# Retention, experts and feed-forward in one kernel: where the operands of the last six row tiles are made

## Chip, core and metric

One core of a Trainium2 chip runs the whole kernel. The metric is the device time of one execution in microseconds; the median of three runs before the change is 1802.8 us (1802.75 to 1803.73).

## What is computed

```python
# q, k, v: (4, 8, 576, 64)   retention with a decay per head
ret = (q @ k.T / 8) * Dmat            # Dmat[i, j] = gamma_h ** (i - j) for i >= j, else 0
x = (ret @ v), heads side by side     # (2304, 512)
# experts: w_gate (512, 8), w1 (8, 512, 1024), w2 (8, 1024, 512)
P = exp(x @ w_gate - max); 8 times: rows, then columns of P are brought to sum
out = sum over e of P[:, e] * (relu(x @ w1[e]) @ w2[e])
# feed-forward, 512 -> 2048 -> 512
h = out @ w_in;  result = max(0.01 * h, h) @ w_out
```

## The kernel before

**Two phases.** The retention walks through 20 chunks (lines 834 to 901): two batch pairs, five row chunks of 128, 128, 128, 128 and 64 rows, two batch halves. The loop behind it runs over 20 units of 512 hidden columns (16 of the experts, 4 of the feed-forward), and in each over three stages of 384 row pairs (three row tiles). A row tile j is a pair of 128-row blocks, one of each half; there are nine, index 0 to 8, and the ninth is put together from the 64-row chunks. Stage 0 takes tiles 0 to 2, stage 1 tiles 3 to 5, stage 2 tiles 6 to 8.

**Products with seven terms.** A block product of 2 by 2 is made from seven products instead of eight, each in three fp16 terms (high by high, high by low, low by high). So each row tile needs seven operands (four blocks of x and three sums), each as a high and a low fp16 part; `PROD` (line 40) names them 0 to 6, and `H_ORDER` (line 41) sets the order of the products of a stage, which take the operands in the order 0, 3, 6, 1, 5, 2, 4. `product_h` (L1028) makes the hidden part, in two column groups g of seven products each; the second products (L1199, L1241 for the first unit) trail and begin after the second stage.

**One step of the retention** (lines 838 to 900), for chunk n: GpSimd decays q of chunk n+2 (L671); TensorE makes the scores of chunk n+1 (`emit_qk`, L694), which VectorE decays (L697); TensorE adds the state's part (L711); `emit_scale` of chunk n-1 sums the absolute values of each row with products against ones (L754) and one more product of a single row that adds 2^-90 (L755), then VectorE makes a power of two of it (L765) and scales the output (L767) into a tile `op`; TensorE adds the chunk's own part (L721), ScalarE takes absolute values (L725); TensorE makes the state's increase (L739), ScalarE copies it (L744). The chunks of 64 rows (n = 8, 9, 18, 19) make no state, and those that open a batch pair (n = 0, 1, 10, 11) use none.

**Operands in the retention.** `emit_operands` (line 805) makes all of a tile in large pieces over the following steps: four sums (L816 to L819, on GpSimd, for tile index 7 on VectorE), two ScalarE casts (L824, three and four operands) and two VectorE subtractions (L826). Tiles 0 to 2 go straight into the operand ring in SBUF; tiles 3 to 7 go into a tile `xt` and by one DMA to DRAM (`keep_x`, L486). Only tile 8 goes through `operand_tasks` (line 515), a list of 14 small tasks: two of GpSimd (L532, L533 and L538, L539), and four times a high part (ScalarE or VectorE, L64), a low part (VectorE, L561) and a store.

**The ring.** It holds eight operands. The first stage's seven lie there from the start; `try_loads` (line 499) loads the next one (L510) when a place is free, all three tiles are stored, and the planner's clock is `LAND` = 4 us past the store. A place comes free after the second column group's product. `need_x` (line 1386) forces tasks and loads that are still missing when a product needs them.

**What sets the order.** In the retention it is written out by hand: `step()` (line 858), four times a chunk from chunk 4 on, issues at most one task of the first unit's W1 (`prep_steps`, line 188). In the loop the class `Order` (line 67) keeps six queues ("evac", "turn", "gate", "hid", "weights", "f64") and a planner's clock; `pump` issues what is ready in that order, "turn" before "weights". An engine's own instructions run in the order of issue; all DMAs go through SyncE's one queue, where one that waits holds those behind it.

**Weights.** A unit's raw W1 and W2 (1 MB each, `load_raw`, L186) are measured by ScalarE (L201), brought to a common power of two, scaled (L261) and split: high parts by ScalarE (L276, L305), sums and low parts by GpSimd (L286, L293, L311). For the first unit the maximum over the partitions is taken by products (`top` and `scale`, L234 and L245), and W1's second low parts are VectorE's (L311); W2 of the first unit is left to the loop. Later units go through VectorE transposes (`quarters`, `beside`, `turned`, `spread`). `float64_steps` (line 394) turns the feed-forward's float64 weights into float32 in the background of the loop; its first loads (L402) start when the ninth tile's four pieces are stored.

## Time and profile before

| what | value |
|---|---|
| median of 3 runs | 1802.8 us |
| profiled execution, its own time | 1801.8 us |
| its span | 1799.9 us |
| mean granted TensorE clock | 0.993 |
| TensorE matmul busy | 1765.2 us (98%) |
| VectorE, ScalarE, GpSimd busy | 83%, 71%, 45% |
| first product of the loop (L1028) | at 91.80 us |

The span runs from the first to the last instruction on the core; the execution's time has 1.9 us around it. Matmuls are pipelined and their ends are modelled, so TensorE's pace is read from the distance of two starts and not from busy time. A row of the order of time gives start, length, engine, line and what ended the idle time before it.

### The profile page before, as it was taken

To read this page: it belongs to the slowest core of one execution; us is meant where nothing else is said; L and a number is where in the kernel's file an instruction comes from. 1 tells how busy PE (TensorE), PEld (TensorE's weight loads), DVE (VectorE), ACT (ScalarE), POOL (GpSimd) and SP (SyncE) were. 2 spreads that over 40 slices of the span, in tenths; PEclk is the share of its full clock that TensorE was granted. 3 is DMA by queue.
4 is the path that set the end of the run, shared out by engine and by line. 5 is a ranking of instruction groups with operands and counts; after the bars stand their busy time and mean duration, and the time that the engine had idled before them with its cause. 6 is when DMAs were issued, how large, how long until landed. Compare 5 with 4: busy or idle time off the path is not lost.

```text
span 1799.9 us, 35885 instructions
## 1 busy us (share of the span) xinstructions
PE 1765.2 (98%) x13686; PEld 1290.1 (72%) x13686; DVE 1489.9 (83%) x2642; ACT 1285.3 (71%) x2808; POOL 815.8 (45%) x782
## 2 busy tenths in 40 slices
PE   9999999999999999999999999999999988999998
PEld 8855677777777777777777777777776555777776
DVE  7955898999888888888898888887776895788886
ACT  6777777777777777777777777777675666877653
POOL 4815362726344463626263444636224972443600
PEclk9999999999999999999999999999999999999999
DMA  9773545446354454454464454443443454444242
GB/s 345 271 252 103 152 127 170 136 150 187 115 171 138 156 156 152 127 170 151 135 190 120 163 147 156 147 143 102 140 150 103 158 170 129 131 125 141 78 128 83
DMA packets 206784, 272.98 MB, mean 152 GB/s; under 512 B 13698, under 2 KB 177556, under 8 KB 201492
## 3 DMA queue, kind: packets, MB, share of 16 engines
q1 hardware_dynamic: 206612, 270.70, 47.9%
q8 instruction: 107, 1.75, 0.4%
q14 instruction: 65, 0.53, 0.1%
HBM read 241.02 MB, written 29.63 MB: 150 GB/s over the span
## 4 chain that ended last, share of the span: by engine, by line
PE 88%; DVE 7%; POOL 2%; issue 1%; ACT 1%; DMA 1%; SPq 0%; DVEq 0%; POOLq 0%; ACTq 0%
PE s L1199 17%; PE hA L1028 12%; PE hB L1028 12%; PE hE L1028 12%; PE s1a L1199 11%; PE s1b L1199 11%; PE hD L1028 6%; PE s L1241 2%; PE s1a L1241 1%; PE s1b L1241 1%; DVE y L1212 1%; DVE xst L561 1%; POOL y L1338 1%; DVE hs L1119 0%; PE xo L721 0%
## 5 line engine op out<-in xcount | busy, mean ns | idle before, releaser
L1028 PEld LDWEIGHTS <-w 128*128 128x128 f16 x5040 | 492.5, 98 | 265.7 <-DMA xring<-x 3.9
L1199 PEld LDWEIGHTS <-hs 128*128 128x128 f16 x3888 | 380.9, 98 | 87.7 <-DVE hs L1119 4.7
L1199 PEld LDWEIGHTS <-hp 128*128 128x128 f16 x2916 | 285.6, 98 | 80.9 <-issue 2.9
L286 POOL TENSOR_TENSOR w<-raw,w 128x384 f16<-128x384 f32 x152 | 163.3, 1088 | 364.1 <-ACT w L276 363.8
L293 POOL TENSOR_TENSOR raw<-raw 128x256 f32<-128x256 f32 x304 | 280.4, 922 | 20.0
L1212 DVE SCALAR_TENSOR_TENSOR y<-s,fac,y 128x256 f32<-128x256 f32 (+1 forms) x322 | 197.6, 614 | 101.2 <-PE s L1199 84.1
L1028 PE MATMUL hE<-xring,w 128*128 128x384 f16 x1440 | 274.7, 326 | 5.3 <-DMA xring<-x 2.1
L1028 PE MATMUL hA<-xring,w 128*128 128x384 f16 x1440 | 276.5, 328 | 2.8 <-ACT w L276 2.3
L1028 PE MATMUL hB<-xring,w 128*128 128x384 f16 x1440 | 274.0, 326 | 0.0
L1199 PE MATMUL s<-w,hs 128*128 128x256 f16 x1932 | 264.2, 273 | 0.8 <-ACT s L1217 0.7
L1119 DVE TENSOR_TENSOR hs<-fs,hs 128x768 f16<-128x768 f32 (+1 forms) x228 | 241.4, 1062 | 8.3 <-ACT hs L1109 6.8
L311 POOL TENSOR_TENSOR w<-raw,w 128x512 f16<-128x512 f32 x148 | 200.4, 1368 | 76.5 <-ACT w L305 76.2
L1109 ACT ACTIVATE hs<-fs 128x768 f16<-128x768 f32 (+1 forms) x228 | 187.6, 823 | 44.4 <-DVE fs L1144 35.1
L446 POOL TENSOR_TENSOR f<-f,e 128x256 f32<-128x256 f32 x64 | 52.8, 825 | 352.5 <-DVE e L438 296.2
L1109 ACT ACTIVATE hp<-fp 128x384 f16<-128x384 f32 x240 | 160.4, 677 | 13.3 <-DVE fp L1067 12.5
L1212 DVE SCALAR_TENSOR_TENSOR y<-s1a,fac,y 128x256 f32<-128x256 f32 (+1 forms) x161 | 98.7, 613 | 50.9 <-ACT s L1217 28.7
L1199 PE MATMUL s1a<-w,hs 128*128 128x256 f16 x972 | 133.4, 273 | 4.6 <-ACT hs L1109 2.4
L1028 PE MATMUL hD<-xring,w 128*128 128x384 f16 x720 | 136.6, 326 | 1.1 <-ACT hD L1056 1.1
L1212 DVE SCALAR_TENSOR_TENSOR y<-s1b,fac,y 128x256 f32<-128x256 f32 (+1 forms) x161 | 98.7, 613 | 43.3 <-ACT s L1217 18.6
L1199 PE MATMUL s1b<-w,hs 128*128 128x256 f16 x960 | 132.1, 273 | 1.8 <-DVE hs L1119 1.4
L1199 PE MATMUL s1a<-w,hp 128*128 128x256 f16 x972 | 132.6, 273 | 1.1 <-DVE y L1212 1.0
L1199 PE MATMUL s1b<-w,hp 128*128 128x256 f16 x960 | 131.6, 274 | 0.5 <-DVE y L1212 0.5
(215 smaller groups left out, 2699.4 us busy)
## 6 DMA issues: line engine op xcount, KB each, us to landing
xring<-x SPq DMA_DIRECT2D x413, 384.0 KB
raw<-in_wm SPq DMA_DIRECT2D x32, 1024.0 KB
r<-in_wf SPq DMA_DIRECT2D x64, 256.0 KB
qk<-in_qk SPq DMA_DIRECT2D x16, 512.0 KB
vk<-in_vk SPq DMA_DIRECT2D x16, 512.0 KB
wf_s<-f SPq DMA_DIRECT2D x32, 256.0 KB
raw<-wf_s SPq DMA_DIRECT2D x8, 1024.0 KB
x<-xst SPq DMA_DIRECT2D x30, 256.0 KB
```

Source lines behind the costliest of these rows:

```text
L286: nc.gpsimd.tensor_tensor(v[0], v[1], v[2], op=ALU.subtract)
L293: nc.gpsimd.tensor_tensor(o, x, y_, op=ALU.subtract)
L311: (nc.gpsimd if u or part else nc.vector).tensor_tensor(lo, r, hi, op=ALU.subtract)
L446: nc.gpsimd.tensor_tensor(dst, dst, cur["tx"].bitcast(F32), op=ALU.mult)
L561: nc.vector.tensor_tensor(st[d][:, :, 1], src[d](), st[d][:, :, 0], op=ALU.subtract)
L1028: nc.tensor.matmul(bank, w[:, a, wi, k, :], x[:, :, b, k, :], start=r in (1, 5) and k == q == 0, stop=k == 1 and q == 2, skip_group_check= ...
L1109: nc.scalar.activation(hid[k][:, 0, a:b], src[:, a:b], AF.Relu if moe and relu else AF.Copy)
L1119: nc.vector.tensor_tensor(t[:, 1, a:b], src[:, a:b], t[:, 0, a:b], op=ALU.subtract)
L1199: nc.tensor.matmul(out_, t[:, a, i, ts], w[:, b, wi, 0, :], start=start and k == 0, stop=k == 5, skip_group_check=True)
L1212: nc.vector.scalar_tensor_tensor(out_, bank, f, out_, op0=ALU.mult, op1=ALU.add)
L1241: nc.tensor.matmul(bank, t[:, a, i, ts], w[:, b], start=l == g == q == 0, stop=l == g == 1 and q == 2, skip_group_check=True)
L1338: nc.gpsimd.tensor_scalar(y[i], y[i], st["s", j][:, h:h + 1], None, op0=ALU.mult)
```

## The change

It keeps the retention's outputs of tiles 3 to 8 in the tiles `y` of the final sum (allocated before the retention for these six), makes the operands of tiles 3 to 7 through `operand_tasks` in small pieces, of which `step()` issues one at every second call, and leaves the rest to the loop's queue "turn". The product of a single row gives way to a bias in ScalarE's absolute value. W1's and W2's maximum of the first unit goes the way of the later units, W1's second low parts go to GpSimd, and `step()` now issues W2's tasks too, with a closer pace for GpSimd and VectorE. The stores of tiles 0 to 2 from the ring wait until chunk 15. The next unit's raw weights load without waiting for stores, and the float64 steps start when all six tiles are stored.

```diff
         def total(p):
             def f():
-                nc.vector.reduce_sum(st["m"][:, p] if u == 0 else m32[:, p], st["mx"][:, p], axis=AX.X)
+                nc.vector.reduce_sum(m32[:, p], st["mx"][:, p], axis=AX.X)
             return f
...
-        def top(p):
-            def f():
-                bk = small_bank(f"wt{u}_{p.start}")
-                n = p.stop - p.start
-                for i in range(n):
-                    nc.tensor.matmul(bk[:1, P * i:P * i + P], st["m"][:, p.start + i:p.start + i + 1], ident,
-                                     start=i == 0, stop=True, skip_group_check=True)
-                nc.vector.reduce_max(st["r"][:, p], bk[:1, :n * P].rearrange("p (a i) -> p a i", a=n), axis=AX.X)
-            return f
-
         def scale(p):
             def f():
-                if u:
-                    bk = st["m"][:, p]
-                else:
-                    bk = small_bank(f"ws{u}_{p.start}")[:, p]
-                    nc.tensor.matmul(bk, ones[:1, :], st["r"][:, p], start=True, stop=True)
-                pow2(st["s"][:, p], bk, f"w{u}_{p.start}")
+                pow2(st["s"][:, p], st["m"][:, p], f"w{u}_{p.start}")
...
@@ -308,7 +292,7 @@
         def low_t(part, g, h):
             def f():
                 r, hi, lo = top_part(part, g, h)
-                (nc.gpsimd if u or part else nc.vector).tensor_tensor(lo, r, hi, op=ALU.subtract)
+                nc.gpsimd.tensor_tensor(lo, r, hi, op=ALU.subtract)
...
         def scaled(p, mx_, key):
             t_ = add("D", 10, total(p), mx_, key)
-            if u == 0:
-                t_ = add("D", 300, top(p), (t_,), key, None, 0.6)
-                return add("D", 500, scale(p), (t_,), key, None, 1.2)
             t_ = add("D", 150, quarters, (t_,), key)
...
-            return [add("G" if u or part else "D", 512, low_t(part, g, h), (ht[h],), key) for h in range(2)]
-
-        after = lambda part, last, key: add(None, 0, lambda: load_raw(u + 1, part), tuple(last), key, lat=0.5, cond=landed)
+            return [add("G", 512, low_t(part, g, h), (ht[h],), key) for h in range(2)]
+
+        after = lambda part, last, key: add(None, 0, lambda: load_raw(u + 1, part), tuple(last), key, lat=0.5, cond=landed if u else None)
...
-        tasks = [Task(None, 0, begin, key="f64", cond=lambda: len(pieces["kept"]) >= 4)]
+        tasks = [Task(None, 0, begin, key="f64", cond=lambda: len(pieces["kept"]) >= 4 * (NJ - NT_S))]
...
+    ypool = ctx.enter_context(tc.tile_pool(name="ypool", bufs=1))
+    y = {i: ypool.tile([P, DM], F32, name=f"y{i}") for i in range(2 * NJ) if i % NJ >= NT_S}
...
+        tiny = aconst.tile([P, 1], F32, name="tiny")
...
@@ -699,7 +683,7 @@
         def place(n, m):
             _, c, half = chunks[n]
-            return (m + 2) % NP if half and c < 4 else m
+            return (m + 2) % NP if half and tile_no(n) < NT_S else m
...
-            nc.scalar.activation(ab[:, :, :w], xov, AF.Abs)
+            nc.scalar.activation(ab[:, :, :w], xov, AF.Abs, bias=tiny)
...
             for m in range(NP):
-                nc.tensor.matmul(l1, ones_b, ab[:, m, :w], start=(m == 0), stop=False, skip_group_check=True)
-            nc.tensor.matmul(l1, ones_b[0:1, :], tiny_b[0:1, :w], start=False, stop=True, skip_group_check=True)
+                nc.tensor.matmul(l1, ones_b, ab[:, m, :w], start=(m == 0), stop=m == NP - 1, skip_group_check=True)
             if c < 4:
-                if half == 0:
-                    xs_t[j] = awk.tile([P, 7, 2, P], F32, tag="op", name=f"op{j}")
-                xv = xs_t[j][:, 2 * half:2 * half + 2].rearrange("p s k i -> p (s k) i")
+                if j >= NT_S:
+                    xv = y[half * NJ + j].rearrange("p (m i) -> p m i", m=NP)
+                else:
+                    if half == 0:
+                        xs_t[j] = wsp.tile([P, 7, 2, P], F32, tag="w1", bufs=4, name=f"op{j}")
+                    xv = xs_t[j][:, 2 * half:2 * half + 2].rearrange("p s k i -> p (s k) i")
...
             j = tile_no(n)
-            if j == 8:
+            if j >= NT_S:
...
                 a11, a12, a22, a21 = (op[:, i] for i in range(4))
-                e = nc.vector if j == 7 else nc.gpsimd
+                e = nc.gpsimd
...
             elif stage == 1:
                 if part == 0:
-                    xt_t[j] = (xring[:, :7, j] if j < NT_S else
-                               awk.tile([P, 7, 2, 2, P], F16, tag="xt", name=f"xt{j}"))
+                    xt_t[j] = xring[:, :7, j]
...
             if stage == 2 and part == 1:
-                kept.append((n + 3, j, xt_t[j]))
+                kept.append((max(n + 3, 13), j, xt_t[j]))
...
-        pre = prep_steps(0, lambda name: bank_a(name) if misc[0] else idle_bank(name))
+        pre = prep_steps(0)
         wait, drain, popped = [0], [], {}
-        PACE = {"G": 3, "D": 4}
+
+        def defer(j):
+            xs = [y[h * NJ + j].rearrange("p (m i) -> p m i", m=NP) for h in range(2)]
+            operand_tasks(0, j, xs, (), (0, j // NT_S), turn_last)
+
+        PACE = {"G": 2, "D": 3}
...
             def step():
                 wait[0] += 1
+                order.t = 0.95 * wait[0]
                 if n < 4:
                     return
+                if wait[0] % 2:
+                    for x in order.queues["turn"][:16]:
+                        if (x.cond is None or x.cond()) and all(
+                                d in popped and wait[0] - popped[d] >= (4 if d.eng == "G" else 2) for d in x.deps):
+                            order.queues["turn"].remove(x)
+                            popped[x] = wait[0]
+                            order.emit(x)
+                            break
                 for x in pre[:16]:
                     if x.eng in PACE and wait[0] - popped.get(x.eng, -9) < PACE[x.eng]:
                         continue
-                    if x.key == (0, "w1", 1) and all(
-                            d in popped and wait[0] - popped[d] >= (6 if d.eng == "G" else 2 + (x.n in (300, 500)))
-                            for d in x.deps):
+                    if all(d in popped and wait[0] - popped[d] >= (4 if d.eng == "G" else 2) for d in x.deps):
                         pre.remove(x)
                         popped[x] = popped[x.eng] = wait[0]
-                        x.f()
-                        x.done = 0.0
+                        order.emit(x)
...
             if n == 13:
                 recip2(inv_of(0), inv_of(0))
             step()
+            if n >= 3 and chunks[n - 2][2] and NT_S <= tile_no(n - 2) < 8:
+                defer(tile_no(n - 2))
         keep_row(N - 2)
-        emit_operands(N - 3, 2, 1)
...
-        misc[0], wait[0] = None, 0
+        wait[0] = 0
+        for n in range(N - 2, N):
+            if tile_no(n) < 8 and chunks[n][2]:
+                defer(tile_no(n))
...
-    ypool = ctx.enter_context(tc.tile_pool(name="ypool", bufs=1, reuse_waits="tile"))
-    y = [ypool.tile([P, DM], F32, name=f"y{i}") for i in range(2 * NJ)]
+    ypool2 = ctx.enter_context(tc.tile_pool(name="ypool2", bufs=1, reuse_waits="tile"))
+    y.update({i: ypool2.tile([P, DM], F32, name=f"y{i}") for i in range(2 * NJ) if i % NJ < NT_S})
```

## Rows read from the trace of the kernel before

**Rows 1.** Stretches: length, busy us of PE, PEld, DVE, ACT, POOL; granted clock; DMA.
```profile
48.60:61.00 12.40, 10.38 (x171) 9.39 (x167) 11.98 (x21) 10.52 (x31) 10.85 (x10) 1.00 1.04 369
61.00:77.60 16.60, 16.60 (x250) 15.10 (x246) 15.49 (x23) 12.10 (x32) 13.85 (x15) 1.00 0.81 314
77.60:91.40 13.80, 12.29 (x142) 10.25 (x140) 13.45 (x21) 7.28 (x15) 10.75 (x12) 0.73 0.20 68
...
400.00:600.00 200.00, 200.00 (x1536) 150.09 (x1535) 173.97 (x305) 150.03 (x326) 99.97 (x97) 1.00 0.48 146
```

**Rows 2.** TensorE in order of time, 42.9 to 96 us.
```profile
43.02 0.68 PE L694 MATMUL sc<-qk 64*64 64x64 f32 x16
...
45.66 1.16 PE L694 MATMUL sc<-qk 64*128 64x128 f32 x16
...
48.64 1.16 PE L694 MATMUL sc<-qk 64*128 64x128 f32 x16
...
61.02 1.16 PE L694 MATMUL sc<-qk 64*128 64x128 f32 x16
...
63.43 0.22 PE L755 MATMUL l<-tiny_b,ones_b 1*128 1x128 bf16 x1
63.58 1.09 PE L721 MATMUL xo<-w,vk 128*64 128x128 f32 x16
...
65.07 1.16 PE L694 MATMUL sc<-qk 64*128 64x128 f32 x16
...
81.16 0.32 PE L694 MATMUL sc<-qk 64*64 64x64 f32 x2
82.99 0.68 PE L694 MATMUL sc<-qk 64*64 64x64 f32 x14 [1.51 <-DVE w L697]
...
90.12 0.61 PE L932 MATMUL hB<-ones_b 128*128 128x512 bf16 x1
...
91.80 1.17 PE L1028 MATMUL hA<-xring,w 128*128 128x384 f16 x3
...
94.21 1.18 PE L1028 MATMUL hE<-xring,w 128*128 128x384 f16 x6
```

**Rows 3.** TensorE's waits, 0 to 92 us: total us, times, longest.
```profile
PE l L754 <- ACT ab L725: 2.0, 2, 1.0
```

**Rows 4.** VectorE's groups, 48.6 to 91.4 us: count, busy us, mean ns.
```profile
L826 DVE TENSOR_TENSOR xt<-op,xt 128x768 f16<-128x768 f32 (+1 forms) x8 | 13.3, 1664 | 0.0
...
L311 DVE TENSOR_TENSOR w<-raw,w 128x512 f16<-128x512 f32 x2 | 2.4, 1208 | 0.0
```

**Rows 5.** All engines in order of time, 96 to 106.5 us (the ninth tile's pieces).
```profile
96.23 0.84 POOL L532 TENSOR_TENSOR sa<-tailx 128x256 f32<-128x256 f32 x1 [7.41 <-DVE tailx L767]
...
99.39 1.10 DVE L561 TENSOR_TENSOR xst<-sa,xst 128x512 f16<-128x512 f32 x1
...
101.35 0.68 DVE L561 TENSOR_TENSOR xst<-sb,xst 128x512 f16<-128x512 f32 x1
...
106.20 0.54 SPq L510 DMA_DIRECT2D xring<-x  x1
```

**Rows 6.** TensorE in order of time, 101 to 120 us.
```profile
102.28 1.14 PE L1028 MATMUL hE<-xring,w 128*128 128x384 f16 x6
103.26 0.65 PE L1028 MATMUL hB<-xring,w 128*128 128x384 f16 x3
...
104.65 1.14 PE L1028 MATMUL hA<-xring,w 128*128 128x384 f16 x6
...
108.96 1.14 PE L1028 MATMUL hA<-xring,w 128*128 128x384 f16 x6
112.24 1.15 PE L1028 MATMUL hE<-xring,w 128*128 128x384 f16 x6 [2.14 <-DMA xring<-x]
...
118.85 1.30 PE L993 MATMUL s1b<-wg_s,xring 128*128 128x16 f16 x46
```

**Rows 7.** One line's instructions: count, shortest/median/longest ns, first and last start.
```profile
L532 POOL TENSOR_TENSOR sa<-tx x9: 718/765/912, 1380.6 to 1476.5; 128x256 f32<-128x256 f32 x9
```

More of the change, by code (lines that the diff above doesn't have):

```diff
@@ L186, in load_raw, with prep_steps @@
             nc.sync.dma_start(raws[u, part], src[:, 2048 * part:2048 * part + 2048])
-    def prep_steps(u, small_bank):
+    def prep_steps(u):
         st = {}
@@ L194, in begin @@
             st["m"] = small.tile([P, 2], F32, tag="m1f", name=f"m{u}")
-            st["r"] = small.tile([1, 2], F32, tag="mrw", name=f"mr{u}", bufs=2)
             st["s"] = small.tile([P, 2], F32, tag="s12", name=f"s{u}")
@@ L598, in retention_moe_ffn_kernel @@
         gq_t = aconst.tile([P, 4 * (S - CH[0][1])], F32, name="gq_t")
-        tiny_b = aconst.tile([1, P], BF16, name="tiny_b")
+        tiny = aconst.tile([P, 1], F32, name="tiny")
         state = [aconst.tile([P, NP, P], F32, name=f"state{i}") for i in range(2)]
@@ L651, in retention_moe_ffn_kernel @@
             nc.tensor.matmul(wu[:, :P], ones_b, ones_b, start=True, stop=True)
-        nc.vector.memset(tiny_b, 2.0 ** -90)
+        nc.vector.memset(tiny, 2.0 ** -90)
         nc.vector.memset(ones, 1.0)
@@ L1435, in retention_moe_ffn_kernel @@
             if u + 1 < NU:
-                w_all[:] = w_all[-120:] + prep_steps(u + 1, idle_bank)
+                w_all[:] = w_all[-120:] + prep_steps(u + 1)
                 order.queues["weights"] += [x for x in w_all if x.key[0] == u + 1]
```

## The prediction, made before the change was run

> **What bounds the kernel now.** I read the stretches first, then TensorE's order of time, then its waits and VectorE's groups. In the long loop a stretch of 200 us holds 200 us of TensorE at granted clock 1.00, with VectorE at 174 us (87%) [rows 1]: there TensorE is the limit, so whatever shortens the way into the loop passes to the end, and whatever makes a hole in the loop is paid in full. The retention before it is different. From 48.6 us to the loop's first product VectorE is busy for 11.98 + 15.49 + 13.45 = 40.9 us of 42.8 (96%) [rows 1]. Between 61 and 77.6 us TensorE still goes at its own pace: a step (one chunk) takes 65.07 - 61.02 = 4.05 us [rows 2]. On either side it does not: it waits twice for ScalarE's absolute values, 2.0 us in all, early in this stretch [rows 3], and at 81.16 us it stops for VectorE's decayed scores [rows 2], after which the granted clock averages 0.73 [rows 1].
>
> The profiled execution took 1801.8 us (span 1799.9), the median of the runs is 1802.8. The sum goes against 1801.8 and its difference is put on the median.
>
> **What the change does, and the step rule.** Counting through the new rule (one task of the "turn" queue at every second call of `step()`, so two per chunk, from chunk 10 on; 14 tasks per tile) 20 of the 70 piece tasks of tiles 4 to 8 go out inside the retention: all of tile 4 (index 3) and 6 tasks of the next. 50 are left for the loop, beside the last tile's 14 that are there already. Of the first unit's 63 weight tasks 48 go out in the retention, so W1 is all but done and W2's scale is known when the loop starts.
>
> **VectorE's load.** Removed from 48.6 to 91.4 us: eight subtractions of L826, 13.3 us, and two of L311, 2.4 us, which GpSimd takes [rows 4]; four sums of tile 8 too (small, no credit taken). Added: nine pieces by my count of the order's choice of engine (four high parts, five low parts). A low part took 1.10 us beside GpSimd's sums and 0.68 us without them [rows 5]; at 1.10 us that is 9.9 us, at 0.68 us 6.1 us. I take 9, because GpSimd is busy most of that time (10.85 of 12.4 us, 13.85 of 16.6) [rows 1]. The load falls by some 6.7 us, to 34 us. That is enough for TensorE's floor, not for much more: between 61 and 77.6 us VectorE was 93% busy [rows 1] and TensorE kept its pace.
>
> **The sum, in order of time.**
>
> 1. Up to 48.6 us: operands of tiles 1 to 3 stay, VectorE stays the limit. The one-row products vanish, but so far only TensorE's slack grows. The maximum of W1 now goes through two VectorE transposes and eight small ScalarE copies in place of two pairs of products. Nothing; between a gain of 0.6 us (four one-row products in the early steps) and a loss of 2 us (each hand-over between VectorE and ScalarE of the length of one wait in [rows 3], twice).
> 2. Steps 10 to 12, 48.64 to 61.02 us: the two waits for ScalarE are 2.0 us [rows 3] and three one-row products go, each worth the distance of its start to the next one's, 63.58 - 63.43 = 0.15 us [rows 2]. ScalarE loses the casts of these tiles but keeps W1's scaling and splitting. At most 2.5 us, at least 0.3; I take 1.3, about half, since half of ScalarE's work there stays.
> 3. Steps 13 to 17, 61.02 to 81.16 us: TensorE at its floor, so five one-row products count whole, 0.75 us (0 if the pieces keep VectorE late, 1.1 if two slower steps also come down).
> 4. Steps 18 and 19, 81.16 to 90.12 us: 8.96 us [rows 2]. The same two steps of the first half, 8 and 9, took 48.64 - 43.02 = 5.62 us [rows 2], of which 1.16 us was the next chunk's scores, which step 19 does not have, and 0.3 us were one-row products: 4.2 us. At most 4.8 us; at least the named stop, 1.5 us. I take 4.0: what made TensorE late, two L311, one tile's sums and two L826, is gone from VectorE, and only W2's scale and two pieces come in.
> 5. From the warming products at 90.12 us to the second loop product at 94.21 us: 4.09 us [rows 2]. In steps 8 and 9 the same small products with no stop before them show no such stretch; the average of 0.73 [rows 1] says that after the stop at 81 us the clock stood for a part at the lower of its two levels, 1.2 of 2.4 GHz. At the upper level the stretch would be half as long. Between 0 and 2.05 us; I take 1.5, because the stop goes.
> 6. In the loop W2's maximum used two pairs of products. One made a loop product last 104.65 - 103.26 = 1.39 us in place of 103.26 - 102.28 = 0.98 [rows 6]: 2 x 0.41 = 0.8 us, gained whole.
> 7. The second stage of the loop, tiles 4 to 6. Now it loses 118.85 - 108.96 = 9.89 us less seven products of 0.98: 3.0 us, for loads of operands [rows 6]. These tiles lie in DRAM long before; what is late is the load, issued at 106.20 us behind the stores of tile 9 and two loads of the float64 steps [rows 5], 6.0 us before the product that waited (112.24) [rows 6]. The change takes the float64 loads away from there (they begin only when all six tiles are stored) and puts the pieces in. From the loop's start, T, eight tasks of one tile and fourteen of the next are to be done. One tile took 5.8 us from its first sum at 96.23 us to the end of its last low part [rows 5], so 8.7 us; 4 us until the planner takes the store as landed (LAND); 6 us for the load: T + 18.7. The product that needs the last-made operand is the third of the stage, now at 91.80 to 108.96 = 17.2 us plus two, and some 2.3 us earlier with terms 5 and 6: T + 17. The queue of SyncE adds to it: that load of 106.20 us left 4 us after the last low part's end (101.35 + 0.68) [rows 5], behind the stores, and there are six stores more now. I put the loss at 4 us, so 1.0 us worse; from 0 (3 us gained) to 9 (6 us lost).
> 8. Later: more pieces in the first 40 us of the loop. From 200 us of loop TensorE lost nothing with VectorE 87% and ScalarE 75% busy (150 of 200) [rows 1]; that is the cover, and if it goes, TensorE waits for its banks. W2's scale and the next unit's raw weights come earlier, which frees ScalarE there. The stores of tiles 1 to 3 move past several loads in SyncE's queue, from chunks 5 to 9 to chunk 15 and on: DMA is at 1.04 of its engines before 61 us, 0.81 and 0.20 after [rows 1], so they are covered. Nothing, up to 2 us lost if GpSimd, which now also has W1's low parts, is late with the next unit's weights.
>
> Sum: -1.3 - 0.75 - 4.0 - 1.5 - 0.8 + 1.0 = -7.35 us. 1801.8 - 7.3 = 1794.5 for such an execution, **1795.5 us** on the median. The likeliest case's own range is 1791 to 1799. What can be told from no change is about 0.2%, 3.6 us: faster means below 1799.2.
>
> **Rivals.**
>
> *Retention stays VectorE's.* The added pieces are the kind of subtraction that is slow beside GpSimd (1.10 against 0.68 us), and the order's rule gives most high parts to VectorE too, since ScalarE was the last booked. Then steps 10 to 17 keep their length (0.3 us gained), the stop at 81 us alone goes (1.5), half a microsecond of clock, 0.8 for W2's products, 1.0 lost in stage two: 2.1 us, 1800.7. Against it: 13.3 + 2.4 us go, and 9.9 at most come. Chance 0.15. The Trainium skill, "SBUF — State Buffer", section "Who interferes with whom", says that a VectorE instruction with two SBUF inputs and a GpSimd instruction that reads SBUF block each other, whichever starts first, for the whole instruction. The two low parts agree with it in direction: the one of 99.39 us began inside a GpSimd sum and took 0.42 us more [rows 5]. By the rule all nine pieces would be paid at the longer price, 9.9 us for the 9 taken.
>
> *The second and third stages starve (slower).* Nine tiles of this kind at the layer change came 95.9/8 = 12 us apart [rows 7], where they wait for finished sums too. Let a tile take p us. The second stage then waits 1.57 p + 10 - 17 us, the third 3 p - 19 more (three tiles, against a stage of 15 us and 4 us of lead), in place of 3.0 now. Against 8.35 us of gains it is slower by over 0.2% from p = 9 on; at p = 10 the waits are 8.7 + 11, so +8.3 us: 1811. Place: TensorE at the first products of stage two and three, waiting for loads. For it: the stores wait on VectorE in SyncE's one queue, and the planner forces all tasks of the stage at once when its first operand is missing. Against: the isolated tile's 5.8 us. Chance 0.10.
>
> *Stage two loses its holes.* If the operands of the fifth and sixth tile are stored by T + 12, the loads, no longer behind float64 loads, come in time: 3.0 us gained rather than 1.0 lost, and with steps 10 to 19 nearer their floors (2.0 + 0.9 + 4.5 + 2.0 + 0.8) 13.2 us: 1789.6. Chance 0.14.
>
> **Numbers.** Forecast 0.61, retention unchanged 0.15, starved 0.10, holes gone 0.14. Faster is the first and the last, 0.75; same 0.15; slower 0.10. The range 1788.5 to 1802 leaves out the starved case, a little of the second and the tail below: under 0.2.
>
> **What would show it.** L755, L826 on tiles past the third, and the products L234 and L245 are gone. Right: the first L1028 product near 84 us in place of 91.80; steps of 3.9 us between 52 and 75 us; no stop before the last chunk's scores; a granted clock near 1.00 from 78 us on. Term 7 is right if TensorE's waits for xring loads in stage two add to 2 to 6 us. Wrong: score products still waiting for L697 near the end of the retention, a first product after 88 us, or a wait for xring of over 10 us in stages two or three together.

## The result, and the profile after

The changed kernel takes **1815.1 us** (median of 6 runs) against 1803.3 for the kernel before on the same chip: ratio 1.0066, 95% interval 1.0053 to 1.0079. It is 11.9 us slower, where 7.3 us faster was forecast; the time lies above the range. The profiled execution took 1817.2 us (span 1815.4), 2.0 above its median. From the gate's first product (L948) to the end it takes 1650.3 us, and 1648.4 before, so nearly all of the loss has happened by that product, which is the milestone below.

| | before | after |
|---|---|---|
| profiled execution, span (us) | 1801.8, 1799.9 | 1817.2, 1815.4 |
| first loop product L1028 | 91.80 | 92.52 |
| second stage's logits L993 | 118.85 | 122.70 |
| first W2 product L1241 | 126.89 | 132.50 |
| gate's first product L948 | 151.53 | 165.12 |

The third stretch of [rows 1], of the kernel after (length; busy us of PE, PEld, DVE, ACT, POOL; granted clock; DMA share, GB/s):

```profile
77.60:91.40 13.80, 9.18 (x102) 8.12 (x97) 5.22 (x13) 4.76 (x16) 7.15 (x9) 0.70 0.43 146
```

VectorE is busy 5.22 us in place of 13.45, in part because work is gone from there as the change meant it, in part because it stands behind the same stop as TensorE (in run 1 below, without that stop, it is busy 10.22). TensorE did less too (9.18 against 12.29), at no better a clock. TensorE in order of time says why (start, us, then the idle time before it in brackets and what ended it):

```profile
75.15 0.68 PE L678 MATMUL sc<-qk 64*64 64x64 f32 x16
...
83.25 1.12 PE L678 MATMUL sc<-qk 64*64 64x64 f32 x16 [4.62 <-DMA qk<-in_qk]
84.31 1.97 PE L695 MATMUL xo<-qd,state 128*128 128x64 f32 x8
```

The last chunk's scores wait 4.62 us for their own input, and what follows goes at the lower clock: the products of L695 take 1.97 us there. SyncE's queue in the same time shows who stood ahead of that load:

```profile
66.34 0.38 SPq L607 DMA_DIRECT2D qk<-in_qk  x1
...
67.28 5.16 SPq L467 DMA_DIRECT2D x<-xring  x3
72.55 2.11 SPq L760 DMA_DIRECT2D s_dram<-s  x1
...
75.71 1.15 SPq L607 DMA_DIRECT2D qk<-in_qk  x1
```

The three stores of the first three tiles (index 0 to 2, 896 KB each), which the change moves here, hold the queue for 5.16 us, and the small store behind them waits another 1.7 us for one of them to land. So the last load of scores (256 KB) is issued at 75.71 us, and at 70.53 us in run 1, where the stores are back. It is used 7.5 us after its issue; in run 1 such loads landed after 6.0 and 6.4 us. So most of the delay is the queue's; the DMA engines, 1.07 to 1.09 busy from 72 to 80 us, add 1.1 to 1.5 us by this comparison. In the loop TensorE then loses more (its longest waits there):

```profile
110.84 1.15 PE L1028 MATMUL hE<-xring,w 128*128 128x384 f16 x6 [1.01 <-DMA xring<-x]
115.07 2.08 PE L1028 MATMUL hB<-xring,w 128*128 128x384 f16 x6 [3.08 <-ACT hB L1038]
...
127.63 1.14 PE L1028 MATMUL hB<-xring,w 128*128 128x384 f16 x6 [1.61 <-ACT hB L1038]
...
139.04 2.08 PE L1028 MATMUL hA<-xring,w 128*128 128x384 f16 x6 [5.08 <-DMA xring<-x]
```

Two kinds of wait stand here. One is for the ring's loads, 1.01 us in the second stage and 5.08 at the start of the third. The other is for banks that ScalarE has not copied out. A product with 2.08 us in place of 1.14 runs at the lower level of the clock: after the stop at 115.07 us three products come 1.9 us apart in place of 0.98, 2.8 us more, about as much again as the stop. The engines' waits from 90 to 146 us (us in all, times, longest):

```profile
ACT fs L1010 <- DVE hs L1119: 6.9, 3, 3.3
DVE xst L64 <- DMA x<-xst: 6.8, 3, 3.5
ACT xst L64 <- DMA x<-xst: 2.9, 3, 2.2
```

VectorE and ScalarE wait for a free staging buffer (xst, four of them), that is, for a store that has not landed. Both engines go through their work in order, so what stands behind such a piece is late too. How that reaches the banks in the second stage shows best beside the kernel before. There:

```profile
119.82 0.55 DVE L1119 TENSOR_TENSOR hs<-fs,hs 128x384 f16<-128x384 f32 x1
...
120.46 0.49 ACT L1010 ACTIVATE fs<-hD 128x384 f32<-128x384 f32 x1 [1.48 <-DVE hs L1119]
```

After:

```profile
100.54 0.29 DVE L64 CAST xst<-y 128x256 f16<-128x256 f32 x1 [3.02 <-DMA x<-xst]
...
112.20 1.43 POOL L519 TENSOR_TENSOR sb<-y,y 128x256 f32<-128x256 f32 x1
...
112.98 1.07 DVE L1119 TENSOR_TENSOR hs<-fs,hs 128x384 f16<-128x384 f32 x1
...
114.14 0.49 ACT L1010 ACTIVATE fs<-hD 128x384 f32<-128x384 f32 x1 [3.34 <-DVE hs L1119]
114.53 0.48 ACT L1038 COPY hB<-hA 128x384 f32<-128x384 f32 x1
```

`fs`, the values taken from bank hD, has one buffer. ScalarE cannot fill it again before VectorE has read it (L1119), and ScalarE's copy for bank hB stands behind it. VectorE comes to L1119 late: it stood 3.02 us for a staging buffer and has then worked, pieces among the rest, with hardly a gap. Beside GpSimd's sums L1119 itself takes 1.07 us in place of 0.55. So the stop of 3.08 us at 115.07 hangs on VectorE, through ScalarE; no run gave `fs` a second buffer.

### The profile page after: what moved, and what is told of

Read it like the earlier page. It is cut to its first block, busy times and chain, and to the rows that moved or that the text cites. A ratio compares the mean times of both kernels' runs of the same rounds, so it can differ in the third digit from the quotient of the medians.

```text
span 1815.4 us, 35893 instructions
## 1 busy us (share of the span) xinstructions
PE 1768.2 (97%) x13658; PEld 1290.0 (71%) x13658; DVE 1488.8 (82%) x2657; ACT 1288.4 (71%) x2827; POOL 823.4 (45%) x790
## 4 chain that ended last, share of the span: by engine, by line
PE 86%; DVE 7%; DMA 2%; ACT 2%; issue 1%; POOL 1%; SPq 0%; DVEq 0%; ACTq 0%; POOLq 0%
PE s L1199 17%; PE hA L1028 12%; PE hB L1028 12%; PE hE L1028 11%; PE s1a L1199 11%; PE s1b L1199 11%; PE hD L1028 6%; PE s L1241 2%; PE s1a L1241 1%; DVE y L1212 1%; DVE xst L542 1%; PE sc L678 1%; DMA qk<-in_qk 1%; PE s1b L1241 1%; DVE hs L1119 1%
## 5 line engine op out<-in xcount | busy, mean ns | idle before, releaser
L1028 PEld LDWEIGHTS <-w 128*128 128x128 f16 x5040 | 494.7, 98 | 279.2 <-issue 19.2
L1028 PE MATMUL hA<-xring,w 128*128 128x384 f16 x1440 | 277.6, 329 | 8.1 <-DMA xring<-x 5.1
L1028 PE MATMUL hB<-xring,w 128*128 128x384 f16 x1440 | 276.0, 328 | 5.1 <-ACT hB L1038 5.1
L1028 PE MATMUL hE<-xring,w 128*128 128x384 f16 x1440 | 276.7, 328 | 3.9 <-ACT w L289 2.1
L1119 DVE TENSOR_TENSOR hs<-fs,hs 128x768 f16<-128x768 f32 (+1 forms) x228 | 241.9, 1064 | 8.7 <-ACT hs L1109 7.2
L295 POOL TENSOR_TENSOR w<-raw,w 128x512 f16<-128x512 f32 x152 | 205.8, 1368 | 78.5 <-ACT w L289 73.5
L1212 DVE SCALAR_TENSOR_TENSOR y<-s1a,fac,y 128x256 f32<-128x256 f32 (+1 forms) x161 | 98.6, 613 | 51.7 <-ACT s L1217 29.1
L1028 PE MATMUL hD<-xring,w 128*128 128x384 f16 x720 | 136.8, 326 | 1.1 <-ACT hD L1056 1.1
```

The source lines that it names most:

```text
L295: nc.gpsimd.tensor_tensor(lo, r, hi, op=ALU.subtract)
L1028: nc.tensor.matmul(bank, w[:, a, wi, k, :], x[:, :, b, k, :], start=r in (1, 5) and k == q == 0, stop=k == 1 and q == 2, skip_group_check= ...
L1119: nc.vector.tensor_tensor(t[:, 1, a:b], src[:, a:b], t[:, 0, a:b], op=ALU.subtract)
L1212: nc.vector.scalar_tensor_tensor(out_, bank, f, out_, op0=ALU.mult, op1=ALU.add)
```

## The experiments

Times are medians; each ratio is to the kernel before on the same chip (1802.0 to 1802.5 us), with its 95% interval. Runs 1, 2 and 13, each with the edits of the one ahead of it, make a ladder from the changed kernel back to the old time: 1815.1, 1811.3, 1804.85, 1802.3 us. The chips differ, so the ratios are the safer comparison: 1.0066, 1.0048, 1.0013, 0.9997.

**1. The stores of the first three tiles back at their places.**

```
-                kept.append((max(n + 3, 13), j, xt_t[j]))
+                kept.append((n + 3, j, xt_t[j]))
```

> The changed kernel, but the ring stores of tiles 0 to 2 go out where they did before (chunks 5 to 9), not in a row at chunk 15. Theory (the three stores of 0.9 MB hold the last score load in SyncE's queue and on the DMA engines): TensorE's wait for qk (4.6 us at 78.6 us) and the half clock behind it go, the loop's first product comes at 86 to 87 us in place of 92.5, and the median falls by 5 to 6 us, to about 1809.5. Rival (the piece stores themselves fill the DMA): the wait stays, 1815. A second rival: the loop starts earlier but its stages wait longer for the same pieces, so that 1 to 2 us of it are left, 1813 to 1814.

Measured: 1811.28 us, 1.0048 [1.0033, 1.0063], 3.9 us better; the intervals of the two ratios just overlap, so the trace has to carry it. The stop before the last scores is gone, the clock is 1.00 from 61 to 91.4 us, and the first loop product comes at 84.03 us, 8.5 earlier than in the changed kernel's profile. (Runs 6 and 12 below leave these stores where the change put them: the stop there is 2.56 and 3.70 us in place of 4.62, and the first loop product at 90.13 and 91.92, so 6 to 8.5 us.) At the first W2 product (128.29) 4.2 of it are left; the loss begins in the first stage (several engines in order of time):

```profile
86.64 0.36 SPq L186 DMA_DIRECT2D raw<-in_wm  x1
...
87.42 4.35 SPq L768 DMA_DIRECT2D inv<-s_dram  x2
91.83 6.70 SPq L467 DMA_DIRECT2D x<-xst  x6
95.89 0.29 DVE L64 CAST xst<-y 128x256 f16<-128x256 f32 x1 [6.33 <-DMA x<-xst]
96.58 0.62 ACT L64 CAST xst<-sa 128x512 f16<-128x512 f32 x1 [6.05 <-DMA x<-xst]
97.17 2.08 PE L1028 MATMUL hE<-xring,w 128*128 128x384 f16 x6 [3.68 <-DVE fp L1067]
```

VectorE stands 6.33 and ScalarE 6.05 us for a staging buffer; TensorE stands behind them, since VectorE's read of its bank (fp, L1067) comes after the piece. Two things are ahead of the stores that would free the buffers: the inverse scales' loads, which wait 4.35 us in SyncE's queue, and 1 MB of the second expert's raw weights, which the change also loads early.

**2. And a piece at every call of `step()`, not at every second.**

```
-                if wait[0] % 2:
+                if True:
```

> As e1, and in the retention a piece task goes out at every call, not at every second, so that about 20 more of the piece tasks are done before the loop. Theory (stages two and three of the loop starve because the pieces are too late): TensorE's waits there, some 7 us in stage two and 8 in stage three with the half clock, fall to half or less, 6 to 9 us below e1, about 1802. Rival (VectorE and ScalarE become late in the retention instead): the first loop product comes 3 to 5 us later than in e1 and the sum is within 2 us of e1.

Measured: 1804.85 us, 1.0013 [1.0003, 1.0022], 6.4 us better, on the same chip; the time is near what was expected. The third stage no longer waits for the ring. The second stage's two stops fall only from 5.94 to 3.80 us, the first stage still stops for 5.05 us, and the first loop product comes 2.1 us later than in run 1.

**3, 4. Single parts on the old schedule.** The kernel before with the one-row products alone removed (their 2^-90 as the bias of the absolute value), and the changed kernel with tiles 4 to 8 made in the retention as before (and all stores as before), so that W1's low parts on GpSimd, the first W2 and the closer pace are left of it.

```
-            nc.scalar.activation(ab[:, :, :w], xov, AF.Abs)
+            nc.scalar.activation(ab[:, :, :w], xov, AF.Abs, bias=tiny)
```

> The kernel before with the one-row products alone taken out (bias in ScalarE's absolute value). Theory: 0.15 us for each of the products where TensorE sets the pace: 1.5 to 3 us faster, 1800.5 to 1801.8. Rival (VectorE sets the pace, or the bias makes ScalarE late): same as before, 1803, or 1 us slower.

> The changed kernel with the operands of tiles 3 to 7 and all stores as before; what stays of the change: no one-row products, W1's and W2's maximum without products, W1's low parts on GpSimd, W2's tasks in the retention, the earlier raw load. Theory (the loss is the late pieces and the bunched stores, and the rest is good by a few us): 1798 to 1801, faster than before by 2 to 5 us. Rival (the weights' tasks in the retention or the earlier raw load cost): 1805 or more.

Measured: 1802.6 us, 1.0000 [0.9991, 1.0010], and 1807.91 us, 1.0031 [1.0021, 1.0042]. Both theories missed; both times are those of the rivals. Without the one-row products the loop does begin 3.1 us earlier (88.68 us), and nothing of it arrives, because the second stage waits for the ring as late as before (GpSimd's first sum of the ninth tile; SyncE's loads; TensorE):

```profile
95.65 0.84 POOL L532 TENSOR_TENSOR sa<-tailx 128x256 f32<-128x256 f32 x1 [7.40 <-DVE tailx L766]
...
105.74 6.31 SPq L510 DMA_DIRECT2D xring<-x  x7
112.28 1.15 PE L1027 MATMUL hE<-xring,w 128*128 128x384 f16 x6 [2.60 <-DMA xring<-x]
```

That product began at 112.24 us before [rows 6], and that sum at 96.23 [rows 5]. The ninth tile's rows come from VectorE, and VectorE is only 0.6 us earlier: as the rival has it, it sets the pace there. Run 4 is a loss: GpSimd is now late in the retention, and the first loop product comes at 93.72 us in place of 91.80:

```profile
81.45 1.13 PE L692 MATMUL xo<-qd,state 128*128 128x128 f32 x8 [1.62 <-POOL w L295]
...
90.76 1.08 PE L692 MATMUL xo<-qd,state 128*128 128x64 f32 x8 [1.12 <-POOL raw L277]
```

The gate's product is 7.3 us late (158.86), so most is lost in the loop: the second stage waits 5.0 us for the ring, 2.14 before. The early raw weights are in this run too, so it does not say which of the weights' edits costs it.

**5, 6, 8, 9. The inverse loads later: three that tried little.** One entry put behind the others in the list of leftovers, on the second run's kernel (5, 8), on the changed kernel (6), and with the pieces' high parts on ScalarE alone besides (9).

```
-                 ]
+                 (14, last_inverse)]
...
-            h = add("AD", 256 * n, high, dep, cond=room)
+            h = add("AD" if layer else "A", 256 * n, (high if layer else lambda: high(nc.scalar)), dep, cond=room)
```

> The stores of tiles 1 to 3 at their old places and a piece at every call, as in the second run, and the two loads of the third stage's inverse scales issued some ten microseconds later, so that the stores of the pieces do not stand behind them in SyncE's queue. Theory (the 5.05 us stall of the fifth bank in the first stage is the staging buffers waiting for stores behind that load): the stall falls below 1.5 us, the half clock at 102 to 108 us (0.64) goes with it, and the kernel takes 1798 to 1801 us, below the kernel before. Rival (there are too few staging buffers, or the DMA engines are full, whatever the order of the queue): the stall comes back within the first or the second stage, and the time stays at 1803.5 to 1806.

> The changed kernel as it is, with the same two loads alone issued later. Theory: its late start (the last score load behind the ring's stores, 4.6 us, and the half clock up to 93 us) stays, the first loop product is still at 92.5 us; the waits for staging buffers after it shrink by 1 to 4 us, so 1810 to 1814. Rival (the queue's order matters only through that late start): 1815, as the changed kernel.

> In the run with the inverse loads late, they were issued only 1.9 us later (91.84 us in place of 89.93) and four stores still stood behind them. Here they are put some 60 calls of the loop later, in the second stage. Theory (SyncE's queue holds the staging buffers back): ScalarE's and VectorE's waits for buffers in the first stage (6.5 and 4.1 us there) fall below 2.5 us, the fifth bank's 4.4 us stall below 1.5 us, and the kernel takes 1797.5 to 1801.5 us. Rival (the pieces come faster than their stores can land, whatever stands in the queue): both waits stay above 3.5 us and the time at 1803 to 1806.

> The kernel of the run before this one, with the high parts of the pieces of the first input on ScalarE alone (before: on whichever of ScalarE and VectorE is freer by the plan). Theory (it is the in-order waits on both engines that hold the banks; with one of them free of buffer waits, the copies of VectorE at least come in time, but ScalarE's copies for the banks wait longer): within 2 us of that run. Rival (VectorE is the bound of the second stage, 5.00 us busy of 5 in the changed kernel): 2 to 5 us faster than that run.

Measured: 1804.5, 1812.42, 1805.04 and 1806.16 us. The number in such an entry is the pause after it, not before it, so the loads moved by one store (91.84 and 91.23 us, from 89.93) in runs 5 and 8, for 14 and for 60 alike. They decide nothing on the queue. Run 6 lies 2.7 us below the changed kernel, but its ratio, 1.0052 [1.0038, 1.0066], overlaps that one's, and in its profile 2.4 us are there already at the first loop product, ahead of the edit, so it may be no difference. Run 9 tells that giving all high parts to one engine does not help (1.0019 [1.0009, 1.0029], against 1.0015 [1.0005, 1.0024] in run 8).

**7. W2 left to the loop.** On run 5's kernel: W1's tasks alone in the retention, at the old pace, and the raw weights held back until the pieces have landed.

```
-        PACE = {"G": 2, "D": 3}
+        PACE = {"G": 3, "D": 4}
...
-                    if all(
+                    if x.key == (0, "w1", 1) and all(
```

> The kernel of the run with the inverse loads late, with the first expert's W2 left to the loop and W1's pieces at the old pace (three and four calls apart), as in the kernel before. Theory (making W2 ahead is worth about what was forecast, 0.8 us, and the closer pace takes room on ScalarE and GpSimd at the end of the retention): within 1.5 us of that run, either way. Rival (W2's place decides the second stage, because its pieces lie on the engines that drain the banks there): 3 us or more slower than that run, with new waits for the banks at 108 to 130 us.

Measured: 1814.68 us, 1.0070 [1.0056, 1.0084], 10.2 slower than run 5. The rival holds, and over a longer stretch than it named: W1 is not ready at the loop's start, and W2 not at the first W2 product.

```profile
94.05 2.08 PE L1031 MATMUL hB<-xring,w 128*128 128x384 f16 x6 [3.89 <-ACT hB L1041]
...
135.15 0.58 PE L1244 MATMUL s1a<-w,hp 128*128 128x512 f16 x1 [4.04 <-ACT w L330]
```

So with the pieces in the loop, the weights have to be made before it. Runs 4 and 7 say that either move without the other loses; with W1's pace and the raw weights in run 7 too, they do not say how much is W2's.

**10, 11, 13, 12. The two things ahead of the stores, apart.** Run 10 is the second run's kernel with the inverse loads behind all pieces' stores; run 11 holds back the raw weights too; run 13 holds back the raw weights alone; run 12 does that in the changed kernel.

```
-        ... cond=landed if u else None)
+        ... cond=landed)
...
-                 (1, lambda: operand_tasks(0, 8, tailx, ...)),
+                 (40, lambda: operand_tasks(0, 8, tailx, ...)),
+                 (1, last_inverse)]
```

> In the two runs before with the inverse loads later, they stood in SyncE's queue only one store further back (issued at 91.84 and 91.23 us, for 3.99 and 3.57 us), so they tried nothing. Here they stand behind the last store of the pieces. Everything else as in the run with a piece at every call. Theory (SyncE's queue holds the staging buffers back): the four stores that were issued from 94.33 us come from about 91 us, the 5.05 us stall of the fifth bank in the first stage falls below 2 us, the clock stays full through 102 to 108 us, and the kernel takes 1798 to 1802 us. Rival (the pieces come faster than their stores land, whatever stands in the queue): a stall over 3.5 us stays, and 1803.5 to 1806.

> As the run before it, and the second expert's first raw weights (1 MB, issued at 89.15 us before) are loaded only once the pieces' stores have landed, as the kernel before has it. Theory of the DMA engines (0.98 busy from 90 to 94 us, so that stores land late): 1 to 3 us faster than the run before it, and the waits for staging buffers fall further. Rival (the stores' landing doesn't decide any more once the queue is free): the same time within 1 us.

> The stores of tiles 1 to 3 back, a piece at every call, the raw weights held back, and the inverse loads where the change has them. Theory (the raw weights decided, and the inverse loads cost little): within 1 us of the run with both, 1801 to 1803. Rival (both had to go): the stall of some 5 us in the first stage returns and 1804 to 1806.

> The changed kernel, with one part undone: the second expert's first raw weights are loaded only once the pieces' stores have landed. Its late start (the last score load, first loop product at 92.5 us) stays. Theory (that load delays the stores that free the staging buffers, in this kernel too): 2 to 5 us faster than the changed kernel, 1810 to 1813, with shorter waits for staging buffers. Rival (in this kernel the stores of tiles 1 to 3 and the slower making of pieces set the buffers): 1814 to 1816.

Measured: 1804.57, 1.0013 [1.0004, 1.0021]; 1801.92, 0.9996 [0.9987, 1.0005]; 1802.3, 0.9997 [0.9988, 1.0006]; 1819.51, 1.0098 [1.0084, 1.0112]. With the queue free but the raw weights ahead, the stop stays (run 10, several engines):

```profile
90.92 0.35 SPq L186 DMA_DIRECT2D raw<-in_wm  x1
...
101.59 0.62 ACT L64 CAST xst<-y 128x512 f16<-128x512 f32 x1 [7.16 <-DMA x<-xst]
102.48 2.08 PE L1030 MATMUL hE<-xring,w 128*128 128x384 f16 x6 [4.98 <-DVE fp L1069]
```

Without the raw weights (run 11) the same piece comes 5 us earlier:

```profile
96.62 0.62 ACT L64 CAST xst<-y 128x512 f16<-128x512 f32 x1 [1.66 <-DMA x<-xst]
```

The four stores ahead of it were issued at nearly the same times in both runs, from 92.3 to 94.9 us in run 10 and from 92.8 to 95.4 in run 11. So it is not the queue but the landing that differs. With the inverse loads where the change has them but no raw weights, the stop is gone too (run 13):

```profile
90.17 2.03 SPq L768 DMA_DIRECT2D inv<-s_dram  x2
92.25 4.73 SPq L467 DMA_DIRECT2D x<-xst  x5
96.24 0.62 ACT L64 CAST xst<-y 128x512 f16<-128x512 f32 x1 [2.66 <-DMA x<-xst]
97.15 1.14 PE L1028 MATMUL hE<-xring,w 128*128 128x384 f16 x6 [0.51 <-DVE fp L1067]
...
104.86 0.29 DVE L64 CAST xst<-tailx 128x256 f16<-128x256 f32 x1 [1.87 <-DMA x<-xst]
...
107.98 1.50 DVE L1119 TENSOR_TENSOR hs<-fs,hs 128x384 f16<-128x384 f32 x1
...
109.58 0.49 ACT L1010 ACTIVATE fs<-hD 128x384 f32<-128x384 f32 x1 [4.27 <-DVE hs L1119]
...
110.50 1.31 PE L1028 MATMUL hB<-xring,w 128*128 128x384 f16 x6 [3.09 <-ACT hB L1038]
```

So my theory of SyncE's queue fell, and the early raw weights are the cause of that stop: 2.55 us (1804.85 to 1802.3), and 2.65 between runs 10 and 11 on one chip. That their 1 MB delays the stores on the DMA engines, which are 0.82 busy from 90 to 96 us in run 10 and 0.58 in run 11, is the reading that fits; only the load's absence was tried. The Trainium skill, "DMA: Bandwidth & Descriptors", section "Issuing engines are not separate DMA queues", says that DMAs, whichever engine starts them, run on the same 16 DMA engines and interleave; the waits of 7.16 and 1.66 us fit that.

In the changed kernel itself the same edit costs 4.4 us (5.8 by the ratios), against both expectations: the pieces are made so late there that the held-back weights (2 MB) come out right ahead of the third stage's ring loads (run 12):

```profile
110.14 18.26 SPq L467 DMA_DIRECT2D x<-xst  x9
...
129.43 0.90 SPq L186 DMA_DIRECT2D raw<-in_wm  x2
130.42 10.89 SPq L491 DMA_DIRECT2D xring<-x  x8
140.37 2.08 PE L1028 MATMUL hA<-xring,w 128*128 128x384 f16 x6 [8.95 <-DMA xring<-x]
```

**14, 15, 16. Another place for VectorE's pieces.** What is left in run 13 is 3.09 us behind the copy for hB, by the same path as in the changed kernel: `fs` waits 4.27 us for L1119, which is late by a wait of 1.87 us for a staging buffer and takes 1.50 us beside GpSimd. Run 14 begins the ninth tile's pieces later (on run 11), run 15 makes more pieces before the loop (a store takes no call of its own), run 16 more still (nor does a sum), both on run 13.

```
                             order.emit(x)
-                            break
+                            if x.eng:
+                                break
...
-                 (1, last_rows),
+                 (14, last_rows),
```

> The run with weights held back and inverse loads late, and the pieces of the ninth tile begun 14 calls of the loop later, so that VectorE makes fewer in the second stage's first half, where ScalarE stood 4.76 us for its low parts and TensorE 3.09 us. Theory (VectorE's load of pieces is the stall): the 3.09 us stall falls below 1.5 us and the kernel takes 1798 to 1801 us. Rival (the wait moves to the third stage's ring loads, which come later by as much): new waits for the ring at 120 to 132 us, 1801 to 1805.

> Stores of tiles 1 to 3 back, a piece at every call, raw weights held back, and a store of a piece no longer uses up a call: a tile takes 10 calls in place of 14, so that about one tile more is made before the loop. Theory (the stall of the second stage is VectorE's pieces there): it falls from 3.09 us to below 1.5 us, retention's steps grow by at most 0.1 us, and 1797 to 1801 us. Rival (VectorE and ScalarE are as full in the last steps of the retention, so that the first loop product comes later by what the second stage wins): 1801 to 1804.

> As the run before it, with GpSimd's sums not using up a call either (8 calls a tile). Theory: 0 to 2 us faster than that run. Rival (GpSimd, which also has W1's and W2's low parts and the decays, is late with these in the last steps, as in the run with the old operands: 1 to 5 us of waits for GpSimd and ScalarE there): 1 to 4 us slower than that run.

Measured: 1805.93, 1.0017 [1.0008, 1.0026]; 1804.75, 1.0016 [1.0007, 1.0025]; 1804.52, 1.0010 [1.0001, 1.0019]. None is better. In run 14 the stop for hB grew to 6.39 us, and the inverse loads came so late that VectorE stood 9.4 us for them, so it does not judge the ninth tile alone. In runs 15 and 16 the stop shrinks to 2.10 and 2.23 us, but the first loop product comes at 88.45 and 92.38 us, from 86.59, and the gate's product at 154.03 and 153.12, from 150.78: what is made earlier makes the retention longer. VectorE by stretches (length, busy; clock; DMA) shows where its work lies. Before:

```profile
50.00:85.00 35.00, 33.44 (x49) 0.99 0.79 293
85.00:105.00 20.00, 18.23 (x33) 0.77 0.48 163
105.00:130.00 25.00, 8.90 (x24) 1.00 0.79 259
```

After:

```profile
50.00:85.00 35.00, 27.82 (x54) 0.97 0.83 284
85.00:105.00 20.00, 13.23 (x30) 0.79 0.41 135
105.00:130.00 25.00, 19.31 (x27) 0.86 0.64 203
```

Run 13:

```profile
50.00:85.00 35.00, 33.59 (x61) 1.00 0.78 269
85.00:105.00 20.00, 15.96 (x34) 1.00 0.62 192
105.00:130.00 25.00, 17.10 (x30) 0.93 0.87 290
```

From 50 to 130 us VectorE has 60.6 us of work before, 60.4 after and 66.7 in run 13. The change moves 10.4 us of it behind 105 us, where the banks' copies also wait. Run 16 brings it back (53.9 of the 55 us before 105 us are busy, 51.7 before the change), and the loop begins as late as in the kernel before. In run 13 VectorE has room by its busy share (15.96 of 20 us, 17.10 of 25) and TensorE stops all the same, so the busy share alone does not explain that stop. No run beats the kernel before; runs 3, 11 and 13 equal it.

## Why the prediction was wrong

**Right in the retention.** Steps of 3.9 us were forecast and 3.89 found (71.26 to 75.15 us after), the one-row products and L826 on late tiles are gone, and with the stores put back the first loop product came at 84.03 us, forecast near 84, with a granted clock of 1.00 from 61 us (run 1). Terms 2 to 5 hold one by one there: gains of 1.14, 1.17, 4.71 and 1.96 us against 1.3, 0.75, 4.0 and 1.5. The nine pieces counted for VectorE are nine in the changed kernel, and take 8.2 us in place of 9.

**Failed: "so they are covered" in term 8.** I took the moved stores as hidden because the DMA engines were 0.81 and 0.20 busy there. I asked for room on the engines that move the data and not for the time that one queue needs to issue it: 5.16 us for three stores ahead of the last loads of the retention. It took 4.62 us on TensorE and the clock after it, and the sign that I had named, a first product after 88 us, came. Undone, it is worth 3.9 us, because part of what it gave back was lost later.

**Failed: term 7's size.** I put the loop's start at 1.0 us worse, at most 6. From the first loop product to the gate's it takes 59.73 us before, 72.60 after, 76.30 in run 1: with the stores aside 16.6 us worse. Of that, making pieces at every second call only costs 9.2 (run 2: 67.12, where 2.1 come back as a later start), the raw weights 2.9 (run 13: 64.19), and 4.5 stay. The rival of the starved stages, with chance 0.10, had the sign, and its place in part: the third stage waits 5.08 us for the ring. But in the second stage these waits, by which I meant to judge term 7, are 1.01 us, under the 2 to 6 I named, and both together 6.1, under the 10 I called wrong. I watched the wrong wait. In run 1 the stops for the ring come to 4.55 us and those at the banks to 9.6 (3.68, 3.36 and 2.58), and of these term 7 has nothing: VectorE and ScalarE, in order, behind a piece that waits for a staging buffer (first stage of run 1), and `fs` behind a late and slower L1119 (second stage). I had named what waits behind SyncE's stores, and never asked what waits behind a piece on the two engines that make it. The sum in term 7 also has a slip: 22 tasks at 5.8 us for 14 are 9.1 us, not 8.7.

**Failed: the premise that what shortens the way into the loop passes to the end.** Run 3 begins the loop 3.1 us earlier and run 13 5.2, and both end like the kernel before. In run 3 the second stage waits for the ninth tile's pieces, stores and loads, which begin with VectorE, and VectorE is no more than 0.6 us earlier; I read the 3.0 us of waits there as a hole of that stage, and not as the place where a gain of TensorE alone ends. In run 13 that wait is gone, and the 4.5 us above, at the banks, take what was won. Whether curing these would bring the forecast gain stays open: no run did.

**Term 8, the raw weights.** I counted their early load as a help for ScalarE. It cost 2.55 us (run 13 against 2). Term 6 put W2's move at 0.8 us; it was not measured by itself. Without the pieces, the weights' part with the early raw weights loses 5.5 us (run 4); beside the pieces its absence, with W1's old pace, loses 10.2 (run 7).

That a low part is longer beside GpSimd was rightly seen: after the change the one at 107.57 us, beside GpSimd's W2 part, took 1.53 us, the one at 120.00 us, with GpSimd idle, 0.68. The Trainium skill, "SBUF — State Buffer", section "Who interferes with whom", says that a VectorE instruction with two SBUF inputs and a GpSimd instruction that reads SBUF contend; these rows agree. What I did not price is that the loop's own subtractions, such as L1119, pay it too once GpSimd makes pieces beside them.

## What to carry to other kernels

Ask of moved work not only whether its engine has room, but what stands behind it in that engine's order when it waits; here a piece waiting for a buffer stopped the banks' copies, a large store on one queue stopped a small load, and a late reader of a single buffer stopped the engine that fills it and all its later copies. Read a transfer's cover from its queue's own timeline too, not from the mean share of the DMA engines alone. And before counting a gain ahead of a loop, ask whether what the next stage waits for comes earlier as well: in run 3 a start 3.1 us earlier changed nothing.

## What was not expected of the hardware

Three stores of 896 KB from the ring held SyncE for 5.16 us, the third alone 3.67, where the two loads of scores ahead of them took 0.37 and 0.38 us. One edit, the raw weights held back, was worth 2.55 us in one schedule and cost 4.4 in another. In the changed kernel the stops of 3.08 and 5.08 us on TensorE were followed by products of 2.08 us in place of 1.14, at a granted clock of 0.50 from 114 to 120 us, the lower of the two levels; the stop of 3.36 us in run 1 (at 110.96 us) was followed by products of 1.14 us. VectorE's L1119 took 0.55 us before, and 1.07 and 1.50 us beside GpSimd's work (changed kernel, run 13).
